# Reordering the opening of a fused spectral-block backward kernel: tables first, half a modulation block first, row scaling on ScalarE, one bias row early

## Chip, cores and metric

One core of a Trainium2 chip. The metric is the device time of one execution in microseconds (us).

## The reference, cut to what matters

The reference computes a block and the gradients of its nine inputs for one `grad_out`. All is bfloat16, S = 2048 rows, D = 512, F = 1792.

```python
mod = (silu(c) @ w_mod)              # six rows of 512: sa, ca, ga, sb, cb, gb
h = layernorm(x) * (1 + ca) + sa
x = x + ga * irfft2(rfft2(h) * (w_r + 1j * w_i))       # spectral part
h = layernorm(x) * (1 + cb) + sb
r = relu(h @ w1 + b1); out = x + gb * (r * r @ w2 + b2) # feed-forward part
# returned: out and the vjp of grad_out for x, w_r, w_i, w1, b1, w2, b2, c, w_mod
```

Two things matter. The gradient of the feed-forward part needs `grad_out @ (w2 * gb).T`, which depends on no row of x. It is ready to be computed as soon as the bias row gb (number 5 of the six) is known. And the spectral part is a chain of stages, each a set of matmuls against transform tables.

## The kernel before

TensorE runs the 224 matmuls `mm<-gT,w2T` of that product as low-priority filler between the stages of the spectral chain. One in-order queue on SyncE (called SPq in the profile) issues all loads, stores and DMA transposes. The opening, with cuts marked:

```python
    for i in range(4):                                   # x rows and the blocks of w_mod
        nc.sync.dma_start(x_sb[:, 4*i:4*i+4, :], x_view[:, 4*i:4*i+4, :])
        if i == 0: load_wm(0)                            # 1 MB: rows 0 and 1
    load_wm(2)
    gT = []
    for b in range(NB):                                  # 4 blocks, but only 2 buffers
        gT.append(w2gp.tile([P, 4, SB], BF16, name="gT", bufs=2))
        for j in range(TB):
            nc.sync.dma_start(gT[b][:, :, j*P:(j+1)*P], g_view[:, TB*b+j, :], transpose=True)
        # [...] w2T after block 0; after block 1 load_wm(1), the 34 loads of w and their write-backs
    build_ta(tc, K, constp, gen, psM)                    # tables
    # [...] the column of silu(c)
    mod_row(1); mod_row(0)
    for q in range(4):                                   # 16 row tiles
        # [...] row statistics
        for j in range(4):
            if j % 2 == 0: nc.vector.tensor_scalar(x_sb[:, t, :], ...)
            else:          nc.scalar.activation(x_sb[:, t, :], ...)
        # [...] h1 = x_sb * ca; first transform psA; its eviction utcs: 1 of 4 on VectorE
    with Priority(tc, LATE):
        nc.sync.dma_start(n1_dram, x_sb)                 # Xs later takes this memory
    build_cd(tc, K, lfp, gen)                            # tables
    for j in (5, 4, 3, 2): mod_row(j)
    # [...] columns of rows 3, 4, 5, then gb2x = 2 * column of row 5
    build_lf(tc, K, lfp, gen)                            # tables LF, most on VectorE
    nc.sync.dma_start(LF_dram, K["LFall"])               # 1.5 MB
    with Priority(tc, LATE):                             # the filler
        for dc in range(4):
            nc.vector.tensor_scalar(w2T[:, dc, :], w2T[:, dc, :], gb2x[:, dc:dc+1], None, op0=ALU.mult)
        # [...] 4 blocks x 14 x 4 matmuls mm<-gT,w2T
    # [...] spectral chain: psB, psC -> Xs (LG transposes of LF_dram between), psG, psT, psY
    nc.sync.dma_start(w1T, B_w1, transpose=True)
    nc.sync.dma_start(w1, w1_view)
    # [...] load_rows(0): second load of x; row statistics; h2T; the feed-forward part
```

Of the kernel before, what the change touches and what calls it, by code (L numbers as in the profile page):

```python
# [9 lines left out]
AF = mybir.ActivationFunctionType  # L10
# [8 lines left out]
D = 512  # L19
# [139 lines left out]



def build_lf(tc, K, cpool, g):
    nc = tc.nc
    V = nc.vector
    ti = g.tile([P, 3], I32, name="lf_ti")
# [9 lines left out]
        V.tensor_scalar(ph[:, i:i + 1], r4, m, a, op0=ALU.mult, op1=ALU.add)  # L175
    sgn = ph[:, 2:3]

    sm = g.tile([P, 6, 4], I32, name="lf_sm")
    nc.gpsimd.iota(sm[:, 0, :], pattern=[[1, 4]], base=0, channel_multiplier=0)
    nc.gpsimd.iota(sm[:, 1, :], pattern=[[-1, 4]], base=3, channel_multiplier=0)  # L180
    nc.gpsimd.iota(sm[:, 2, :], pattern=[[0, 2], [1, 2]], base=0, channel_multiplier=0)
    nc.gpsimd.iota(sm[:, 3, 0:2], pattern=[[1, 2]], base=0, channel_multiplier=0)
    nc.gpsimd.iota(sm[:, 3, 2:4], pattern=[[-1, 2]], base=1, channel_multiplier=0)
    nc.gpsimd.iota(sm[:, 4, 0:2], pattern=[[1, 2]], base=2, channel_multiplier=0)
    nc.gpsimd.iota(sm[:, 4, 2:4], pattern=[[-1, 2]], base=3, channel_multiplier=0)
    mk = g.tile([P, 6, 4], BF16, name="lf_mk")
    V.tensor_scalar(mk[:, 0:5], sm[:, 0:5], sl, None, op0=ALU.is_equal)
    V.tensor_scalar(mk[:, 1], mk[:, 1], sgn, None, op0=ALU.mult)
# [6 lines left out]
    K["LF"] = [LF[:, 2 * gi:2 * gi + 2] for gi in range(8)]  # L195
    K["LFall"] = LF
    for q in range(4):
        kr = g.tile([P, 2, 2, 2, 64], I16, name="lf_kr", bufs=1)
        nc.gpsimd.iota(kr[:, :, :, 0, :], pattern=[[1, 2], [16, 2], [32, 64]], base=2 * q, channel_multiplier=0)
        nc.gpsimd.iota(kr[:, :, :, 1, :], pattern=[[-1, 2], [-16, 2], [32, 64]], base=32 - 2 * q, channel_multiplier=0)  # L200
        if q == 0:
            nc.gpsimd.iota(kr[:, 0, :, 1, 0:32], pattern=[[16, 2], [64, 32]], base=8, channel_multiplier=0)
            nc.gpsimd.iota(kr[:, 0, :, 1, 32:64], pattern=[[-16, 2], [64, 32]], base=56, channel_multiplier=0)
        v = g.tile([P, 2, 4, P], I16, name="lf_v", bufs=1)
        for i in range(2):
            V.tensor_scalar(v[:, i], kr.rearrange("p a h x u -> p (a h) (x u)"), t, ph[:, i:i + 1], op0=ALU.mult, op1=ALU.add)
        if q == 0:
            V.tensor_scalar(v[:, :, 0, 2:64:4], v[:, :, 0, 2:64:4], 512.0, None, op0=ALU.add)
        V.tensor_single_scalar(v, v, 2047, op=ALU.bitwise_and)
        w = g.tile([P, 2, 4, P], BF16, name="lf_w", bufs=2)  # L210
        nc.scalar.activation(w, v, AF.Sin, scale=TWO_PI / 2048, bias=K["npi"])
        n0 = 2 if q == 0 else 0
        for i in range(2):
            for x in range(2):
                V.tensor_tensor(LF[:, 4 * q + n0:4 * q + 4, i, 64 * x:64 * x + 64].rearrange("p n (a b) -> p n a b", b=4),
                                w[:, i, n0:4, 64 * x:64 * x + 64].rearrange("p n (a b) -> p n a b", b=4),
                                mk[:, x, None, None, :].broadcast_to([P, 4 - n0, 16, 4]), op=ALU.mult)
            for h in range(n0):
                V.tensor_tensor(LF[:, h, i, 0:64].rearrange("p (a b) -> p a b", b=4), w[:, i, h, 0:64].rearrange("p (a b) -> p a b", b=4),
                                mk[:, 2 + h, None, :].broadcast_to([P, 16, 4]), op=ALU.mult)  # L220
                V.tensor_tensor(LF[:, h, i, 64:128].rearrange("p (j a b) -> p j a b", j=2, b=2),
                                w[:, i, h, 64:128].rearrange("p (j a b) -> p j a b", j=2, b=2),
                                mk[:, 4, :].rearrange("p (j b) -> p j b", j=2)[:, :, None, :].broadcast_to([P, 2, 16, 2]), op=ALU.mult)
        nc.scalar.activation(LF[:, 4 * q:4 * q + 4, 2, :], LF[:, 4 * q:4 * q + 4, 0, :], AF.Copy, scale=-1.0)
# [4 lines left out]
def spec_f1_row(tc, K, hrow, t, UT, pool, name):  # L229
# [4 lines left out]
        nc.tensor.matmul(ps[:, 2 * c:2 * c + 2, :], lhsT=hrow[:, (c + 2) * P:(c + 3) * P], rhs=K["TA"][:, 1:3], start=False, stop=True)  # L234
    dst = UT[:, :, :, t, :]
    src = ps.rearrange("p c (a b) -> p c a b", b=8)
    if t % 4 == 0:
        nc.vector.tensor_copy(out=dst, in_=src)
    else:
        nc.scalar.copy(out=dst, in_=src)  # L240


def make_ae(nc, pool):
# [190 lines left out]
def kernel(  # L434
# [34 lines left out]
    ccolf = constp.tile([P, 4], FP32, name="ccolf")  # L469
    b1col = constp.tile([P, NFC], FP32, name="b1col")  # L470
    gsc = constp.tile([P, 6, 4], FP32, name="gsc")
    mcol = constp.tile([P, 3, 4], FP32, name="mcol")
    SB_C, CB1_C, GB_C = range(3)
    modb = constp.tile([P, 5, D], BF16, name="modb")
    GA_B, GB_B, CA1_B, CB1_B, SB_B = range(5)
    K = build_basic(tc, constp)
# [9 lines left out]
    nc.vector.memset(ind, 0.0)  # L486
    nc.vector.memset(ind[:, :, 0:1], 1.0)
    gen = tc.alloc_tile_pool(name="gen", bufs=1, side="right")

    gap = tc.alloc_tile_pool(name="gap", bufs=1)  # L490
    gaT = [gap.tile([P, NFC, SB], BF16, name="gab", bufs=4) for b in range(NB)]
# [17 lines left out]
    def load_wm(i):  # L509
        nc.sync.dma_start(wmt[i], wm_view[:, :, 2 * D * i:2 * D * (i + 1)])  # L510

    for i in range(4):
        nc.sync.dma_start(x_sb[:, 4 * i:4 * i + 4, :], x_view[:, 4 * i:4 * i + 4, :])
        if i == 0:
            load_wm(0)
    load_wm(2)
    w2T = w2gp.tile([P, 4, F], BF16, name="w2T")
    gT = []
    for b in range(NB):
# [3 lines left out]
        if b == 0:  # L523
            nc.sync.dma_start(w2T, B_w2, transpose=True)
        if b == 1:
            load_wm(1)
            for gi in range(8):
                nc.gpsimd.memset(Z[gi][:, :, :, DF:FP], 0.0)
                load_w(gi)
                nc.sync.dma_start(wz_dram[:, gi], Z[gi])  # L530
    psF1 = tc.alloc_tile_pool(name="psF1", bufs=2, space=PSUM)
    psM = tc.alloc_tile_pool(name="psM", bufs=2, space=PSUM)
    UT = utcs.tile([P, 4, 16, NT, 8], BF16, name="utcs")
    build_ta(tc, K, constp, gen, psM)
    pv = psM.tile([P, 32], BF16, name="vrow_ps", bufs=1)
    nc.tensor.transpose(pv, vrow, K["ident"][0:32, 0:32])
    nc.vector.tensor_copy(b1col, pv[:, 8:8 + NFC])
    nc.vector.tensor_copy(ccolf, pv[:, 0:4])
    nc.scalar.activation(sigcol, ccolf, AF.Sigmoid)
    sccol = p0.tile([P, 4], BF16, name="sccol")  # L540
    nc.vector.tensor_tensor(sccol, ccolf, sigcol, op=ALU.mult)
    nc.vector.tensor_copy(scf, sccol)
    scb = p0.tile([P, 4, P], BF16, name="scb")
    nc.vector.tensor_copy(scb, sccol[:, :, None].broadcast_to([P, 4, P]))



    srow = p0.tile([1, D], BF16, name="srow")
# [9 lines left out]
        else:  # L558
            nc.scalar.copy(out=srow, in_=ps[0:1, :])

    mod_row(1)
    mod_row(0)


    for q in range(4):
# [8 lines left out]
        nc.vector.scalar_tensor_tensor(out=nb, in0=mv[:, :, 0], scalar=-1.0, in1=i1, op0=ALU.mult, op1=ALU.mult)  # L574
        for j in range(4):
            t = 4 * q + j
            if j % 2 == 0:
                nc.vector.tensor_scalar(x_sb[:, t, :], x_sb[:, t, :], inv1[:, t:t + 1], nb[:, j:j + 1], op0=ALU.mult, op1=ALU.add)
            else:
                nc.scalar.activation(x_sb[:, t, :], x_sb[:, t, :], AF.Identity, bias=nb[:, j:j + 1], scale=inv1[:, t:t + 1])  # L580
# [5 lines left out]

    with Priority(tc, LATE):
        nc.sync.dma_start(n1_dram, x_sb)
    build_cd(tc, K, lfp, gen)
    for j in (5, 4, 3, 2):  # L590
        mod_row(j)
    pm = constp.tile([1, 2], BF16, name="pm")
    nc.vector.memset(pm[:, 0:1], 1.0)
# [10 lines left out]
        for i in range(4):  # L604
            nc.tensor.matmul(psd[:, fs], lhsT=sacol[:, i, e * (i // 2):e * (i // 2) + 1], rhs=K["Cd"][:, i % 2, fs], start=(i == 0), stop=(i == 3))
    nc.vector.tensor_scalar(dcrow, psd, 128.0, None, op0=ALU.mult)
    psc = psM.tile([P, 3, 4], FP32, name="modc_ps", bufs=1)
    for i, row in enumerate((modb[0:1, SB_B, :], modb[0:1, CB1_B, :], modb[0:1, GB_B, :])):
        for cc in range(4):
            nc.tensor.matmul(psc[:, i, cc:cc + 1], lhsT=row[:, cc * P:(cc + 1) * P], rhs=pm[:, 0:1], start=True, stop=True)  # L610
    nc.vector.tensor_copy(mcol, psc)
    gb2x = constp.tile([P, 4], FP32, name="gb2x")
    nc.vector.tensor_scalar(gb2x, mcol[:, GB_C], 2.0, None, op0=ALU.mult)
    build_lf(tc, K, lfp, gen)
    nc.sync.dma_start(Cd_dram, K["Cd"])
    nc.sync.dma_start(LF_dram, K["LFall"])
    gen.release()
# [617 lines left out]
```

## Time and profile before

| | before |
|---|---|
| median of 3 runs | 475.09 us (475.04 to 477.51) |
| span of the profiled execution | 473.4 us |
| TensorE (PE) busy | 432.9 us, 91% |
| VectorE (DVE), ScalarE (ACT) busy | 331.2 us, 257.0 us |
| first filler matmul, last filler matmul | 42.5 us, 137.0 us |

Busy time plus idle time of TensorE is the span, so 473.4 - 432.9 = 40.5 us of idle TensorE is what an edit of the order can win, apart from busy time at a lower clock. A line of a timeline holds start, duration, engine, line, operation; in brackets the idle time just before and what ended it. The prediction shows the opening. Two views also belong here: the stretch 104.6 to 137 us by busy times (length, then PE, PEld, DVE, ACT, POOL, clock, DMA share, GB/s), and the timeline of the loads there (start, duration, engine, line, operation; in brackets the idle time just before and what ended it).

```profile
104.60:137.00 32.40, 28.46 (x179) 15.50 (x172) 21.46 (x46) 22.36 (x40) 0.00 (x0) 1.00 0.49 141
```

### The profile page before, as it was taken

What the parts mean: (1) busy time and instruction counts of PE and PEld (TensorE: products, weight loads), DVE (VectorE), ACT (ScalarE), POOL (GpSimd) and SP (SyncE); (2) the same over time, 40 slices, a digit from 0 to 9 for tenths busy, and PEclk for the clock granted to TensorE, in tenths of its full rate; (3) what the DMA queues carried; (4) which work ended last, traced back from release to release, by engine and by line L of the source; (5) the groups of instructions that cost most, each with busy time, mean ns of one, the idle gap of its engine ahead of it and who ended that gap; (6) DMA issues with size and microseconds to landing.
All of it is one profiled execution on the core that took longest, in us unless ns stands there. A gap on an engine that the chain in (4) does not pass through costs nothing.

```text
span 473.4 us, 7172 instructions
## 1 busy us (share of the span) xinstructions
PE 432.9 (91%) x2485; PEld 218.3 (46%) x2485; DVE 331.2 (70%) x759; ACT 257.0 (54%) x463; POOL 12.7 (3%) x64
## 2 busy tenths in 40 slices
PE   0758999998899999999999798997999999999997
PEld 0434544664454444443454244443555556555442
DVE  5888946983886457677666864733957676769896
ACT  3356745755777148547653764634554546444641
POOL 4121000000000000000000000000000000000000
PEclk9978999999999999999999999998999999999999
DMA  8975667998039639939973696797688549999994
GB/s 275 244 197 163 183 209 222 273 251 300 24 111 370 197 102 208 323 113 172 250 245 115 136 297 232 236 217 240 168 231 292 152 121 317 206 234 292 246 253 137
DMA packets 149371, 101.23 MB, mean 214 GB/s; under 512 B 99282, under 2 KB 133592, under 8 KB 148696
## 3 DMA queue, kind: packets, MB, share of 16 engines
q1 hardware_dynamic: 149336, 100.78, 79.2%
q8 instruction: 19, 0.31, 0.3%
q14 instruction: 16, 0.13, 0.1%
HBM read 35.44 MB, written 41.73 MB: 163 GB/s over the span
## 4 chain that ended last, share of the span: by engine, by line
PE 65%; DVE 11%; DMA 8%; ACT 6%; SPq 5%; issue 2%; POOL 1%; DVEq 0%; ACTq 0%
PE og L803 13%; PE mm L1065 10%; PE mm L780 10%; PE mm L993 10%; PE mm L629 3%; PE psG L302 3%; PE psC L262 2%; PE psT L333 2%; PE psY L347 2%; SPq L770 2%; PE psB L275 2%; DMA o<-gx_dram 2%; DVE l_st L569 2%; DMA n_dram<-x_sb 1%; DMA x<-in_A_x_dram 1%
## 5 line engine op out<-in xcount | busy, mean ns | idle before, releaser
L629 PE MATMUL mm<-gT,w2T 128*128 128x512 bf16 x224 | 54.7, 379 | 2.8 <-DVE gab L632 2.3
L780 PE MATMUL mm<-h2T,w 128*128 128x512 bf16 x224 | 53.3, 379 | 2.2 <-DMA h2T<-h_dram 1.1
L993 PE MATMUL mm<-gab,h_sb 128*128 128x448 bf16 x256 | 52.8, 360 | 0.0
L803 PE MATMUL og<-w,h 128*128 128x512 bf16 x224 | 52.0, 380 | 0.0
L803 PE MATMUL og<-w1T,gab 128*128 128x512 bf16 x224 | 50.3, 379 | 0.0
L1065 PE MATMUL mm<-g_sb,hn 128*128 128x512 bf16 x224 | 50.2, 380 | 0.0
L781 ACT ACTIVATE r<-mm,b1col 128x512 bf16<-128x512 f32 x56 | 37.6, 684 | 13.4 <-PE mm L780 8.6
L993 PEld LDWEIGHTS <-h_sb 128*128 128x128 bf16 x256 | 25.4, 99 | 22.0 <-issue 1.8
L780 PEld LDWEIGHTS <-w 128*128 128x128 bf16 x224 | 21.1, 97 | 30.7 <-issue 8.5
L803 PEld LDWEIGHTS <-gab 128*128 128x128 bf16 x224 | 21.8, 98 | 25.3 <-DVE gab L787 0.5
L629 PEld LDWEIGHTS <-w2T 128*128 128x128 bf16 x224 | 21.2, 97 | 26.4 <-issue 6.8
L1065 PEld LDWEIGHTS <-hn 128*128 128x128 bf16 x224 | 21.5, 98 | 25.5 <-issue 1.3
L803 PEld LDWEIGHTS <-h 128*128 128x128 bf16 x224 | 21.1, 98 | 25.1 <-issue 2.3
L632 DVE CAST gab<-mm 128x512 bf16<-128x512 f32 x28 | 19.2, 686 | 15.1 <-PE mm L629 14.9
L783 DVE TENSOR_TENSOR h<-r 128x1024 bf16<-128x1024 bf16 x28 | 19.3, 690 | 14.2 <-ACT r L781 14.1
L997 ACT CAST gw<-mm 128x448 bf16<-128x448 f32 x16 | 8.5, 532 | 28.5 <-PE mm L993 28.5
L634 ACT CAST gab<-mm 128x512 bf16<-128x512 f32 x28 | 16.3, 582 | 11.3 <-PE mm L629 11.2
L867 ACT CAST o<-og 128x512 bf16<-128x512 f32 x16 | 9.3, 580 | 22.6 <-PE og L803 22.6
L336 ACT ACTIVATE Tsb<-psT 128x512 bf16<-128x512 f32 x32 | 18.3, 601 | 4.9 <-PE psT L333 2.5
L428 DVE SCALAR_TENSOR_TENSOR gm_junk<-wmc,onef,gmbc 128x512 bf16<-128x512 bf16 x24 | 18.0, 750 | 2.9 <-ACT gmbc L417 2.6
L816 ACT CAST G<-og 128x512 bf16<-128x512 f32 x16 | 9.3, 580 | 19.0 <-PE og L803 19.0
L347 PE MATMUL psY<-Tsb,TAT 128*128 128x256 bf16 x128 | 18.1, 272 | 1.5 <-ACT Tsb L336 1.4
(268 smaller groups left out, 763.6 us busy)
## 6 DMA issues: line engine op xcount, KB each, us to landing
h_dram<-h SPq DMA_DIRECT2D x28, 256.0 KB, 3.9
gh_dram<-gab SPq DMA_DIRECT2D x28, 256.0 KB, 4.1
w<-in_B_w_dram SPq DMA_DIRECT2D x2, 1792.0 KB
wm<-in_w_mod_dram SPq DMA_DIRECT2D x3, 1024.0 KB, 6.8
wmc<-in_w_mod_dram SPq DMA_DIRECT2D x12, 256.0 KB, 4.7
out_dram<-gwm SPq DMA_DIRECT2D x12, 256.0 KB, 3.8
wz_dram<-Z SPq DMA_DIRECT2D x8, 258.0 KB, 2.4
xs_dram<-Xs SPq DMA_DIRECT2D x8, 258.0 KB, 2.9
```

Of the source, the lines that this page charges most:

```text
L336: nc.scalar.activation(Tsb, ps, AF.Copy, scale=EF_S)
L347: nc.tensor.matmul(psY[:, H * s:H * s + H], lhsT=K["TAT"][:, s * e], rhs=Tsb[:, H * e:H * e + H], start=(e == 0), stop=(e == 1))
L428: nc.vector.scalar_tensor_tensor(out=junk, in0=wmc[:, i, :], scalar=K["onef"], in1=gmbc, op0=ALU.mult, op1=ALU.mult, accum_out=self.gsc[:, ...
L629: nc.tensor.matmul(ps, lhsT=w2T[:, dc, fc * P:(fc + 1) * P], rhs=gT[b][:, dc, :], start=(dc == 0), stop=(dc == 3))
L632: nc.vector.tensor_copy(out=gaT[b][:, fc, :], in_=ps)
L634: nc.scalar.copy(out=gaT[b][:, fc, :], in_=ps)
L780: nc.tensor.matmul(ps, lhsT=w1[:, dc, (fc + i) * P:(fc + i + 1) * P], rhs=h2T[b][:, dc, :], start=(dc == 0), stop=(dc == 3))
L781: nc.scalar.activation(r[:, i, :], ps, AF.Relu, bias=b1col[:, fc + i:fc + i + 1])
L783: nc.vector.tensor_tensor(h2, r, r, op=ALU.mult)
L803: nc.tensor.matmul(ps, lhsT=lhs(fc), rhs=rhs[:, fc, :], start=(fc == 0 and init is None), stop=(fc == NFC - 1))
L993: nc.tensor.matmul(ps[:, 0:W4], lhsT=h2_sb[:, t, dc * P:(dc + 1) * P], rhs=ghn[t // 4][:, t % 4, fs], start=(t == 0), stop=(t == NT - 1))
L1065: nc.tensor.matmul(ps, lhsT=hns[fc][:, t, :], rhs=g_sb[:, t, :], start=(t == 0), stop=(t == NT - 1))
```

## The change

The intent is to relieve VectorE in the opening and let the filler start sooner. Four parts: the tables are made first of all; of the first w_mod block only the half with row 1 is loaded at first; three of four row scalings and all psA evictions go to ScalarE; row 5 is computed ahead of the other late rows and turned into `gb2x` at once. With them go two smaller edits: row 0, whose half block now lands late, joins the late rows, and the products of row 1 get a higher priority. The core of the diff:

```diff
-    for i in range(4):
+    nc.sync.dma_start(x_sb[:, 0:4, :], x_view[:, 0:4, :])
+    nc.sync.dma_start(wmt[0][:, :, D:2 * D], wm_view[:, :, D:2 * D])
+    for i in range(1, 4):
         nc.sync.dma_start(x_sb[:, 4 * i:4 * i + 4, :], x_view[:, 4 * i:4 * i + 4, :])
-        if i == 0:
-            load_wm(0)
 [...]
         if b == 1:
+            nc.sync.dma_start(wmt[0][:, :, 0:D], wm_view[:, :, 0:D])
             load_wm(1)
 [...]                                  # build_ta, build_cd, iotas of build_lf: before the loads
-            if j % 2 == 0:
+            if j == 0:
                 nc.vector.tensor_scalar(x_sb[:, t, :], ...)
 [...]
-    if t % 4 == 0:
-        nc.vector.tensor_copy(out=dst, in_=src)
-    else:
-        nc.scalar.copy(out=dst, in_=src)
+    nc.scalar.copy(out=dst, in_=src)
 [...]
-    for j in (5, 4, 3, 2):
+    mod_row(5)
+    psc = psM.tile([P, 4], FP32, name="modc_ps", bufs=1)
+    for cc in range(4):
+        nc.tensor.matmul(psc[:, cc:cc + 1], lhsT=modb[0:1, GB_B, cc * P:(cc + 1) * P], rhs=K["ones_col"][0:1, :], start=True, stop=True)
+    gb2x = constp.tile([P, 4], FP32, name="gb2x")
+    nc.vector.tensor_scalar(gb2x, psc, 2.0, None, op0=ALU.mult)
+    for j in (4, 0, 3, 2):
         mod_row(j)
 [...]
-    gb2x = constp.tile([P, 4], FP32, name="gb2x")
-    nc.vector.tensor_scalar(gb2x, mcol[:, GB_C], 2.0, None, op0=ALU.mult)
```

More of the change, by code (lines that the diff above doesn't have):

```diff
@@ L157, in build_cf, with iotas_lf, build_lf @@
     K["Cf"] = Cf
-def build_lf(tc, K, cpool, g):
+def iotas_lf(tc, g):
+    nc = tc.nc
+    sm = g.tile([P, 6, 4], I32, name="lf_sm")
+    nc.gpsimd.iota(sm[:, 0, :], pattern=[[1, 4]], base=0, channel_multiplier=0)
+    nc.gpsimd.iota(sm[:, 1, :], pattern=[[-1, 4]], base=3, channel_multiplier=0)
+    nc.gpsimd.iota(sm[:, 2, :], pattern=[[0, 2], [1, 2]], base=0, channel_multiplier=0)
+    nc.gpsimd.iota(sm[:, 3, 0:2], pattern=[[1, 2]], base=0, channel_multiplier=0)
+    nc.gpsimd.iota(sm[:, 3, 2:4], pattern=[[-1, 2]], base=1, channel_multiplier=0)
+    nc.gpsimd.iota(sm[:, 4, 0:2], pattern=[[1, 2]], base=2, channel_multiplier=0)
+    nc.gpsimd.iota(sm[:, 4, 2:4], pattern=[[-1, 2]], base=3, channel_multiplier=0)
+    krs = []
+    for q in range(4):
+        kr = g.tile([P, 2, 2, 2, 64], I16, name="lf_kr", bufs=4)
+        nc.gpsimd.iota(kr[:, :, :, 0, :], pattern=[[1, 2], [16, 2], [32, 64]], base=2 * q, channel_multiplier=0)
+        nc.gpsimd.iota(kr[:, :, :, 1, :], pattern=[[-1, 2], [-16, 2], [32, 64]], base=32 - 2 * q, channel_multiplier=0)
+        if q == 0:
+            nc.gpsimd.iota(kr[:, 0, :, 1, 0:32], pattern=[[16, 2], [64, 32]], base=8, channel_multiplier=0)
+            nc.gpsimd.iota(kr[:, 0, :, 1, 32:64], pattern=[[-16, 2], [64, 32]], base=56, channel_multiplier=0)
+        krs.append(kr)
+    return sm, krs
+def build_lf(tc, K, cpool, g, sm, krs):
     nc = tc.nc
@@ L176, in build_lf @@
     sgn = ph[:, 2:3]
-    sm = g.tile([P, 6, 4], I32, name="lf_sm")
-    nc.gpsimd.iota(sm[:, 0, :], pattern=[[1, 4]], base=0, channel_multiplier=0)
-    nc.gpsimd.iota(sm[:, 1, :], pattern=[[-1, 4]], base=3, channel_multiplier=0)
-    nc.gpsimd.iota(sm[:, 2, :], pattern=[[0, 2], [1, 2]], base=0, channel_multiplier=0)
-    nc.gpsimd.iota(sm[:, 3, 0:2], pattern=[[1, 2]], base=0, channel_multiplier=0)
-    nc.gpsimd.iota(sm[:, 3, 2:4], pattern=[[-1, 2]], base=1, channel_multiplier=0)
-    nc.gpsimd.iota(sm[:, 4, 0:2], pattern=[[1, 2]], base=2, channel_multiplier=0)
-    nc.gpsimd.iota(sm[:, 4, 2:4], pattern=[[-1, 2]], base=3, channel_multiplier=0)
     mk = g.tile([P, 6, 4], BF16, name="lf_mk")
@@ L197, in build_lf @@
     for q in range(4):
-        kr = g.tile([P, 2, 2, 2, 64], I16, name="lf_kr", bufs=1)
-        nc.gpsimd.iota(kr[:, :, :, 0, :], pattern=[[1, 2], [16, 2], [32, 64]], base=2 * q, channel_multiplier=0)
-        nc.gpsimd.iota(kr[:, :, :, 1, :], pattern=[[-1, 2], [-16, 2], [32, 64]], base=32 - 2 * q, channel_multiplier=0)
-        if q == 0:
-            nc.gpsimd.iota(kr[:, 0, :, 1, 0:32], pattern=[[16, 2], [64, 32]], base=8, channel_multiplier=0)
-            nc.gpsimd.iota(kr[:, 0, :, 1, 32:64], pattern=[[-16, 2], [64, 32]], base=56, channel_multiplier=0)
+        kr = krs[q]
         v = g.tile([P, 2, 4, P], I16, name="lf_v", bufs=1)
@@ L471 @@
     gsc = constp.tile([P, 6, 4], FP32, name="gsc")
-    mcol = constp.tile([P, 3, 4], FP32, name="mcol")
-    SB_C, CB1_C, GB_C = range(3)
+    mcol = constp.tile([P, 2, 4], FP32, name="mcol")
+    SB_C, CB1_C = range(2)
     modb = constp.tile([P, 5, D], BF16, name="modb")
@@ L488 @@
     gen = tc.alloc_tile_pool(name="gen", bufs=1, side="right")
+    psF1 = tc.alloc_tile_pool(name="psF1", bufs=2, space=PSUM)
+    psM = tc.alloc_tile_pool(name="psM", bufs=2, space=PSUM)
+    build_ta(tc, K, constp, gen, psM)
+    build_cd(tc, K, lfp, gen)
+    lf_io = iotas_lf(tc, gen)
     gap = tc.alloc_tile_pool(name="gap", bufs=1)
@@ L530 @@
                 nc.sync.dma_start(wz_dram[:, gi], Z[gi])
-    psF1 = tc.alloc_tile_pool(name="psF1", bufs=2, space=PSUM)
-    psM = tc.alloc_tile_pool(name="psM", bufs=2, space=PSUM)
     UT = utcs.tile([P, 4, 16, NT, 8], BF16, name="utcs")
-    build_ta(tc, K, constp, gen, psM)
-    pv = psM.tile([P, 32], BF16, name="vrow_ps", bufs=1)
-    nc.tensor.transpose(pv, vrow, K["ident"][0:32, 0:32])
-    nc.vector.tensor_copy(b1col, pv[:, 8:8 + NFC])
-    nc.vector.tensor_copy(ccolf, pv[:, 0:4])
-    nc.scalar.activation(sigcol, ccolf, AF.Sigmoid)
-    sccol = p0.tile([P, 4], BF16, name="sccol")
-    nc.vector.tensor_tensor(sccol, ccolf, sigcol, op=ALU.mult)
-    nc.vector.tensor_copy(scf, sccol)
-    scb = p0.tile([P, 4, P], BF16, name="scb")
-    nc.vector.tensor_copy(scb, sccol[:, :, None].broadcast_to([P, 4, P]))
+    with tc.high_priority():
+        pv = psM.tile([P, 32], BF16, name="vrow_ps", bufs=1)
+        nc.tensor.transpose(pv, vrow, K["ident"][0:32, 0:32])
+        nc.vector.tensor_copy(b1col, pv[:, 8:8 + NFC])
+        nc.vector.tensor_copy(ccolf, pv[:, 0:4])
+        nc.scalar.activation(sigcol, ccolf, AF.Sigmoid)
+        sccol = p0.tile([P, 4], BF16, name="sccol")
+        nc.vector.tensor_tensor(sccol, ccolf, sigcol, op=ALU.mult)
+        nc.vector.tensor_copy(scf, sccol)
+        scb = p0.tile([P, 4, P], BF16, name="scb")
+        nc.vector.tensor_copy(scb, sccol[:, :, None].broadcast_to([P, 4, P]))
     srow = p0.tile([1, D], BF16, name="srow")
@@ L559, in mod_row @@
             nc.scalar.copy(out=srow, in_=ps[0:1, :])
-    mod_row(1)
-    mod_row(0)
+    with tc.high_priority():
+        mod_row(1)
     for q in range(4):
@@ L588 @@
         nc.sync.dma_start(n1_dram, x_sb)
-    build_cd(tc, K, lfp, gen)
-    for j in (5, 4, 3, 2):
+    mod_row(5)
[5 more added lines that the diff above has]
+    for j in (4, 0, 3, 2):
         mod_row(j)
@@ L606 @@
     nc.vector.tensor_scalar(dcrow, psd, 128.0, None, op0=ALU.mult)
-    psc = psM.tile([P, 3, 4], FP32, name="modc_ps", bufs=1)
-    for i, row in enumerate((modb[0:1, SB_B, :], modb[0:1, CB1_B, :], modb[0:1, GB_B, :])):
+    psc = psM.tile([P, 2, 4], FP32, name="modc_ps", bufs=1)
+    for i, row in enumerate((modb[0:1, SB_B, :], modb[0:1, CB1_B, :])):
         for cc in range(4):
@@ L611 @@
     nc.vector.tensor_copy(mcol, psc)
-    gb2x = constp.tile([P, 4], FP32, name="gb2x")
-    nc.vector.tensor_scalar(gb2x, mcol[:, GB_C], 2.0, None, op0=ALU.mult)
-    build_lf(tc, K, lfp, gen)
+    build_lf(tc, K, lfp, gen, *lf_io)
     nc.sync.dma_start(Cd_dram, K["Cd"])
```

## The prediction

> **What bounds the kernel now.** I read the page first: PE is busy 91% of a 473.4 us span, so most of the kernel is bound by TensorE, and an edit of the opening can only gain where TensorE is not yet full. The page's 40 slices put that hole in the first 50 us. So I asked next for the busy times by stretch, with borders set at the events that matter. Columns: stretch, its length, busy us and instructions of PE, PEld, DVE, ACT, POOL, then granted clock, DMA share, GB/s.
>
> ```profile
> PE   0758999998899999999999798997999999999997
> 5.40:43.60 38.20, 23.70 (x120) 12.60 (x120) 31.59 (x105) 19.03 (x30) 8.40 (x25) 0.87 0.89 227
> 43.60:57.50 13.90, 11.54 (x70) 6.58 (x70) 12.75 (x44) 8.97 (x13) 1.30 (x4) 1.00 0.61 163
> 57.50:76.10 18.60, 18.24 (x81) 7.61 (x79) 9.47 (x26) 7.70 (x15) 0.35 (x1) 1.00 0.76 269
> 76.10:95.70 19.60, 18.71 (x126) 12.06 (x127) 18.30 (x36) 14.15 (x26) 0.34 (x8) 1.00 0.91 218
> ```
>
> From 5.4 to 57.5 us VectorE is the full engine: 31.59 + 12.75 = 44.3 of 52.1 us, 85%, in a row of small waits. TensorE has 23.7 of the first 38.2, and part of that at half clock. After 57.5 TensorE is full. What fills it is the product gT x w2T (line 629, 224 matmuls): low-priority work with no hurry, stuffed between the stages of the spectral chain. So earlier filler does not by itself end the kernel earlier; the chain beside it has to move too.
>
> That chain I took from the timeline and the chain of waits.
>
> ```profile
> 41.59 0.16 DVE L613 TENSOR_SCALAR gb2x<-mcol 128x4 f32<-128x4 f32 x1
> 46.87 1.28 DVE L624 TENSOR_SCALAR w2T<-w2T,gb2x 128x1792 bf16<-128x1792 bf16 x2
> 57.90 0.33 SPq L616 DMA_DIRECT2D LF_dram<-LF  x1
> 58.41 0.33 SPq L530 DMA_DIRECT2D wz_dram<-Z  x1
> 63.41 5.64 SPq L522 DMA_TRANSPOSE gT<-in_grad_out_dram  x4
> 69.57 0.35 SPq L588 DMA_DIRECT2D n_dram<-x_sb  x1
> 76.13 1.08 ACT L264 CAST Xs<-psC 128x514 bf16<-128x514 f32 x2 [1.30 <-DMA n_dram<-x_sb]
> ```
>
> Read it backwards. At 76.13 the first spectral block leaves PSUM; it had waited for the write of x_sb to DRAM, since Xs lies in memory that x_sb gave up. That write sits in the one in-order DMA queue behind the third block of gT transposes. Those wait for a gT buffer, that is for the first 56 filler matmuls, which end at about 63.4; the queue itself was free from 58.74 on. And the filler starts late because the scaled w2T is complete only at 48.15, as the bias row of g comes last of the six rows. From 76.13 to 95.7 TensorE (18.71 of 19.60) and VectorE (18.30) are both full.
>
> **What the skill says.** The Trainium skill, "VectorE: DVE Perf Modes", section "The perf-mode tier table": a PSUM operand costs a copy a speed tier. The trace agrees: the same 128x512 elements take 684 ns out of PSUM and 415 ns from SBUF. "TensorE: Matmul & The Clock Gate", section "What's actually happening": TensorE falls to half clock after an idle window and needs about 3.4 us of work to leave it. The trace agrees: after the idle stretch from 26 to 30 us the psA matmuls follow each other at 0.21 us, at 24 us they did so at 0.11. "DMA: Bandwidth & Descriptors", section "Measured": 1 MB takes 6.15 us; here the 1 MB blocks of w_mod took 6.8 us to land in the median, among other traffic.
>
> **The change part by part.** Durations are from the groups of the first 60 us.
>
> ```profile
> L578 DVE TENSOR_SCALAR x_sb<-x_sb,inv,l_nb 128x512 bf16<-128x512 bf16 x8 | 3.1, 415 | 0.0
> L238 DVE CAST utcs<-psA 128x512 bf16<-128x512 f32 x4 | 2.7, 684 | 1.2 <-PE psA L234 1.2
> L580 ACT ACTIVATE x_sb<-x_sb,l_nb,inv 128x512 bf16<-128x512 bf16 x8 | 6.1, 805 | 6.3 <-DVE l_nb L574 6.3
> L240 ACT CAST utcs<-psA 128x512 bf16<-128x512 f32 x12 | 6.8, 590 | 7.4 <-PE psA L234 7.2
> ```
>
> Row scaling and evictions: four of eight scalings and all four evictions leave VectorE, 4 x 0.415 + 4 x 0.684 = 4.4 us. ScalarE gets 4 x 0.805 + 4 x 0.590 = 5.6 us; it had 28.0 of 52.1 us busy, so it goes to 33.6, 64%. VectorE goes from 85% to 77%, and now waits more often on ScalarE for a scaled pair.
>
> Tables first: the same instructions, moved. The tables for Cd (4 x 0.37 + 2 x 0.42 = 2.3 us of VectorE, 1.4 of ScalarE) go ahead of the first row scaling, and all index patterns on GpSimd (some 5 us) ahead of the first 1/sqrt. GpSimd stood idle until 8.27, so that costs at most half a us. It removes the waits of the later patterns (16.0 us on GpSimd, off the path).
>
> First w_mod block alone: half a MB less in front of the x rows. At the 345 GB/s of the stretch from 5 to 10 us that is 1.5 us earlier for x, gT and w2T. The half comes back after the second gT block, so the 34 loads of w (one per 0.62 us of queue time in the trace) start at the same time as before, about 29 us. They and their write-backs then take the queue to 57 to 58.5 us, whatever the engines do. This is the new floor.
>
> Bias row early: its four matmuls come second. A walk along the new order of VectorE with the durations above gives: first product h at 16.0 (before: 16.98), the fourth at 24.0 (before: 23.25, here ScalarE is late), the last at 34.65 (before: 36.6), w2T scaled by 36.4 (before: 48.15). Then row 0, whose half block lands only at about 33, holds VectorE until 38.5. The LF tables start at 39.5 instead of 43.6 and end at 52.3 instead of 57.4: 5 us. The filler stands at 44 matmuls at about 55 and reaches 56 at about 57.5.
>
> The queue and the 56th matmul thus meet at about 58. The third gT block goes out at 58.1 instead of 63.4: 5.3 us. The 5.64 of transposes, the 6.4 of the x_sb write, Xs at 70.8. TensorE has 82 filler matmuls in a row for this stretch, 82 x 0.227 = 18.6 us from about 53, so up to 71.6: hardly a gap. Then the 19.6 us to the next stage as before. 160 of the filler matmuls stand ahead of that stage instead of 150, 10 x 0.227 = 2.3 us less for the stretch from 104.6 to 137. There the chain runs through a load of x, row statistics and normalization, so I count a third of it, 0.7. Nothing behind 137 us is touched. Sum: 5.3 + 0.7 = 6.0, and 475.09 - 6.0 = 469.1.
>
> **The rivals.** First, the queue does not hold: the w loads start 1.5 us earlier because the transposes drain earlier, the filler gets its whole lead. TensorE is then some 9 us ahead at 50 us (36 filler matmuls at 0.227 and 8 psB at 0.11), and the kernel takes about 466. For: VectorE loses 4.4 us and w2T is ready 12 us earlier. Against: the loads go out at an even pace in the trace, with the DMA engines at 0.6, which looks like the queue's own issue time.
>
> Second, ScalarE takes VectorE's place. Three scalings of four and all evictions now stand on one in-order engine, a pair of rows costing 2 x 0.59 + 1.5 x 0.8 = 2.4 us, against 22 us for all eight pairs over a window of 25. My walk shows the fourth product already 0.75 us late. If the last product h comes no earlier than 36.6, LF gains only the order of its own work, some 2 us, and the time is about 473.
>
> Third, the new order of the queue: the fourth gT block now stands ahead of the first LG transpose and needs 112 filler matmuls (about 68.5). If it holds LG or shares the engines with the x_sb write, 1 to 3 us go back: about 471.
>
> **Range and chances.** The middle is 469.1. The second and third rival set the upper end, the first the lower: 465.5 to 472.8. Faster by over 2% needs 465.6, that is nearly the whole of the first rival plus the stretch after 104.6: 0.11. Slower by over 2% has no mechanism: 0.01.
>
> **What would show it.** Right: VectorE 4 to 5 us less busy before 57 us; w2T scaled by 37; LF written to DRAM at about 52, or queued behind the w loads to 57; third gT block at 57 to 60 with the queue busy up to it; Xs at 70 to 72; the same distance from Xs to the next stage, 19 to 20 us; everything behind 140 shifted as a whole. Wrong: a third gT block that leaves at 62 or later (the opening did not speed up), a wait of over 2 us of TensorE ahead of Xs, or a stretch after Xs that takes back what the opening gave.

## More of the kernel before

```profile
98.67 8.82 SPq L680 DMA_TRANSPOSE w1T<-in_B_w_dram  x1
107.59 0.52 SPq L657 DMA_DIRECT2D xs_dram<-Xs  x1
108.16 0.42 SPq L683 DMA_DIRECT2D w<-in_B_w_dram  x1
110.77 0.86 SPq L702 DMA_DIRECT2D x<-in_A_x_dram  x2
110.80 0.60 ACT L336 ACTIVATE Tsb<-psT 128x512 bf16<-128x512 f32 x1 [2.39 <-DMA xs_dram<-Xs]
117.26 0.69 DVE L727 TENSOR_TENSOR x<-yg,x 128x1024 bf16<-128x1024 bf16 x1 [2.04 <-DMA x<-in_A_x_dram]
117.99 1.29 DVE L731 BATCH_NORM_STATS2 l_st<-x 128x6 f32<-128x512 bf16 x2
```

TensorE is idle for 32.40 - 28.46 = 3.9 us in the stretch 104.6 to 137 us. The feed-forward part waits for x to be read a second time: that load leaves at 110.77, behind the w1T transposes and the 1.75 MB of w1, and VectorE waits 2.04 us for it. A second link shows here: the last write of Xs leaves at 107.59, also behind w1T. The view of the queue's waits names this write as what held the x load (2.0 us), and ScalarE's first eviction `Tsb` waits 2.39 us for it; TensorE stands 1.41 us behind that eviction, its longest wait in this stretch.

## The result, and the profile after

The changed kernel took 469.69 us in the median (4 runs, 468.04 to 469.82); the kernel before took 475.96 beside it (4 runs). The ratio is 0.9857, 95% interval 0.9819 to 0.9895: within 2%, inside the range, 0.6 us from the predicted 469.1. A ratio here is the mean time of one kernel's runs over that of the other's of the same rounds, so it is not quite the ratio of the quoted medians. The profiled spans are 473.4 and 467.9. Executions over 1.5% slower than the fastest of the same kernel are left out of the means. All outputs are right.

The busy times by stretch after the change (same stretches and columns as before):

```profile
5.40:43.60 38.20, 25.57 (x139) 13.73 (x140) 32.51 (x119) 26.06 (x42) 6.43 (x20) 0.91 0.89 227
43.60:57.50 13.90, 13.18 (x77) 7.09 (x75) 11.89 (x39) 10.21 (x17) 0.35 (x1) 1.00 0.58 158
57.50:76.10 18.60, 16.40 (x76) 7.12 (x75) 6.34 (x10) 6.36 (x11) 0.42 (x8) 1.00 1.04 294
76.10:95.70 19.60, 19.02 (x131) 12.33 (x129) 19.18 (x38) 13.34 (x25) 0.00 (x0) 1.00 1.01 261
104.60:137.00 32.40, 30.96 (x183) 16.66 (x182) 25.78 (x53) 26.06 (x48) 0.00 (x0) 1.00 0.46 160
```

TensorE is busier in the opening and in the last stretch. From 57.5 to 76.1 it has a hole that was not there. VectorE is no less busy up to 57.5 (32.51 + 11.89 = 44.4, before 44.3): it lost 4.4 us of row work and did, in the same time, 2.1 us more of filler evictions and some 3.8 us of table work for a later stage that had come behind 57.5 before. Over the whole kernel it is 325.6, that is 5.6 us less, and ScalarE 263.5, that is 6.5 us more. The row-scaling group of ScalarE shows it (busy us, mean ns, then idle before):

```profile
L589 ACT ACTIVATE x_sb<-x_sb,l_nb,inv 128x512 bf16<-128x512 bf16 x12 | 9.1, 807 | 0.0
```

The w2T scaling from the tile's view (min/median/max ns, first to last start), and the chain to Xs from the timeline:

```profile
L636 DVE TENSOR_SCALAR w2T<-w2T,gb2x x4: 676/677/678, 29.7 to 35.9; 128x1792 bf16<-128x1792 bf16 x4
```

```profile
58.26 0.33 SPq L628 DMA_DIRECT2D LF_dram<-LF  x1
59.14 8.11 SPq L533 DMA_TRANSPOSE gT<-in_grad_out_dram  x4
67.78 0.35 SPq L597 DMA_DIRECT2D n_dram<-x_sb  x1
70.17 6.39 SPq L533 DMA_TRANSPOSE gT<-in_grad_out_dram  x4
74.87 1.08 ACT L270 CAST Xs<-psC 128x514 bf16<-128x514 f32 x2 [2.30 <-DMA n_dram<-x_sb]
```

The scaled w2T is complete at 36.5 (before 48.15), as predicted. The third gT block leaves at 59.14 (before 63.41), but its transposes hold the queue for 8.11 us instead of 5.64, x_sb is written late, and Xs comes at 74.87 instead of 76.13. So only 1.3 us of the opening reached the next stage: psG starts at 94.4, before at 95.7. Yet the filler ends at 129.2, before at 137.0 (start of its last matmul, here and below). The loads behind the chain show where more came from:

```profile
93.55 7.65 SPq L692 DMA_TRANSPOSE w1T<-in_B_w_dram  x1
101.86 0.43 SPq L695 DMA_DIRECT2D w<-in_B_w_dram  x1
105.41 0.81 SPq L714 DMA_DIRECT2D x<-in_A_x_dram  x2
112.70 1.29 DVE L743 BATCH_NORM_STATS2 l_st<-x 128x6 f32<-128x512 bf16 x2
```

The second load of x leaves 5.4 us earlier and its row statistics start 5.3 us earlier. One cause lies in the fence above: the fourth gT block (70.17) now goes out while the queue would wait for the x_sb write anyway. Before, it needed filler matmul 112, which came too late for that, and it stood at 77.56 for 5.1 us between the first LG transpose and the rest. The w1T transposes now leave 5.1 us earlier, and behind them the last write of Xs (101.30 instead of 107.59), for which ScalarE's `Tsb` now no longer waits.

The ledger of idle TensorE, from the busy times (length minus busy; both traces hold the same 2485 matmuls):

| stretch, us | before | after | difference |
|---|---|---|---|
| 0 to 5.4 | 5.4 | 5.4 | 0 |
| 5.4 to 57.5 | 16.9 | 13.4 | -3.5 |
| 57.5 to 76.1 | 0.4 | 2.2 | +1.8 |
| 76.1 to 104.6 | 0.9 | 0.6 | -0.3 |
| 104.6 to 137 | 3.9 | 1.4 | -2.5 |
| 137 to the end | 13.0 | 12.7 | -0.3 |
| all | 40.5 | 35.7 | -4.8 |

Busy time fell by 0.75 (432.93 to 432.18). Together this is the 5.5 us between the spans. A ledger says where time went; it does not say why. That is for the experiments.

### The profile page after: what moved, and what is told of

Same layout as the page of the kernel before. It is cut to its first block, busy times and chain, and to the rows that moved or that the text cites. A ratio compares the mean times of both kernels' runs of the same rounds, so it can differ in the third digit from the quotient of the medians.

```text
span 467.9 us, 7171 instructions
## 1 busy us (share of the span) xinstructions
PE 432.2 (92%) x2485; PEld 218.3 (47%) x2485; DVE 325.6 (70%) x747; ACT 263.5 (56%) x475; POOL 12.2 (3%) x64
## 4 chain that ended last, share of the span: by engine, by line
PE 72%; ACT 7%; DMA 7%; DVE 6%; SPq 6%; issue 2%; POOL 0%; ACTq 0%; DVEq 0%
PE og L815 14%; PE mm L1077 10%; PE mm L792 10%; PE mm L1005 10%; PE mm L641 7%; PE psY L353 3%; PE psG L308 3%; PE psT L339 3%; SPq L782 2%; DMA LG<-LF_dram 2%; DMA o<-gx_dram 2%; PE psC L268 2%; PE psB L281 2%; DMA x_sb<-in_A_x_dram 1%; PE mod_ps L562 1%
## 5 line engine op out<-in xcount | busy, mean ns | idle before, releaser
L795 DVE TENSOR_TENSOR h<-r 128x1024 bf16<-128x1024 bf16 x28 | 19.3, 690 | 12.8 <-ACT r L793 12.7
L799 DVE TENSOR_TENSOR gab<-r,gab 128x1024 bf16<-128x1024 bf16 x28 | 19.2, 685 | 0.0
L1151 ACT CAST gh<-psY 128x512 bf16<-128x512 f32 x16 | 8.6, 593 | 18.4 <-PE psY L353 18.4
```

The lines of the kernel that those rows point to most:

```text
L795: nc.vector.tensor_tensor(h2, r, r, op=ALU.mult)
L799: nc.vector.tensor_tensor(gh, r, gh, op=ALU.mult)
```

## The experiments

All comparisons with the kernel before are on the same chip, five rounds each. They were three calls of four runs, each call on a different chip. There the kernel before took 479.08, 477.62 and 478.82 us in the median, with a spread of 5 to 7 us, so ratios carry an interval of about half a per cent to either side. In the traces of runs 1 to 8, 35 of the 2485 matmul records are missing; I use start times and waits from them, and idle times only to a few tenths. In the edits, ORDER_ONLY stands for a scheduling dependence without a semaphore.

The prediction's own route is the earlier Xs, carried through the chain. After the comparison of the traces two theories stand beside it. In the expectations, A is the filler's head start on TensorE, carried to the end of the filler; the order of the queue is then worth at most 1 us. B is the better place of the fourth gT block in the queue, which the head start makes possible and which brings the loads of w1T and x forward. A rival to all is that VectorE's relief of 4.4 us does it.

### 1. The fourth gT block put back behind the first LG transpose

An order edge in the changed kernel, TensorE's order untouched.

```diff
+        if q == 0:     # gT[3]: its four transposes are to stand behind the first LG transpose
+            [tc.add_manual_dep(g.ins, lg_ins.ins.name, ORDER_ONLY, reason="order") for g in gt_ins[12:16]]
```

> The changed kernel, with the fourth gT block held behind the first LG transpose in the DMA queue, the place it has in the kernel before. TensorE's order is the same instruction for instruction. Theory A (the gain is the filler's head start on TensorE, carried to the end of the filler): at most 1 us lost, about 470. Theory B (the gain is 5.1 us of gT transposes moved out of the queue's busy stretch between the spectral blocks and the second load of x, so that this load comes 5.4 us earlier): the load goes back to about 110 us and 3 to 5 us are lost, about 474.

Measured: 473.77 us (471.16 to 475.09), ratio 0.9882 (0.9828 to 0.9936), span 472.5.

```profile
75.41 5.13 SPq L534 DMA_TRANSPOSE gT<-in_grad_out_dram  x4
96.80 8.90 SPq L695 DMA_TRANSPOSE w1T<-in_B_w_dram  x1
108.74 0.91 SPq L717 DMA_DIRECT2D x<-in_A_x_dram  x2
108.85 0.60 ACT L342 ACTIVATE Tsb<-psT 128x512 bf16<-128x512 f32 x1 [3.17 <-DMA xs_dram<-Xs]
115.71 0.69 DVE L742 TENSOR_TENSOR x<-yg,x 128x1024 bf16<-128x1024 bf16 x1 [0.94 <-DMA x<-in_A_x_dram]
```

Xs and psG came even a little earlier than in the changed kernel (psG 93.5), yet the x load leaves 3.3 us later, VectorE waits for it again, and the filler ends at 132.5 instead of 129.2. TensorE's longest wait is back too: 2.19 us behind `Tsb`, which waits for the last write of Xs (105.80 here, 101.30 in the changed kernel). The granted clock in 104.6 to 137 us is 0.95, in the changed kernel 1.00; by an estimate from these two and the 32.4 us of the stretch, up to 1.6 us of the loss are at the lower clock. So the end doesn't follow Xs, and the place of this block does count: 3 to 4 us in the traces. The timed ratios are less sure: they differ by 0.0025 from the first timing of the changed kernel, inside the interval. This run speaks for B in its mechanism and leaves the size at 1 to 4 us.

### 2. The changed kernel without the early bias row

```diff
-    mod_row(5)
-    [column of row 5 and gb2x here]
-    for j in (4, 0, 3, 2):
+    for j in (5, 4, 0, 3, 2):
         mod_row(j)
+    [column of row 5 and gb2x with the other columns, as in the kernel before]
```

> The changed kernel without the early bias row: the six rows in the order 1, 5, 4, 0, 3, 2 and the scale of w2T taken from the late column product, as before. Theory A: the filler starts at 42 to 44 us as before the change, nearly all of the gain is gone, 474 to 476. Rival (the gain is VectorE's 4.4 us less work in the opening): 471 to 472, since that work is still saved.

Measured: 479.65 us (478.25 to 480.92), ratio 1.002 (0.9973 to 1.0067). The first filler matmul is at 43.5, the third gT block at 63.8, the fourth at 82.3. The other three parts are all there, and nothing is gained: VectorE's relief by itself is refuted as the cause.

### 3. The kernel before with the early bias row alone

```diff
-    for j in (5, 4, 3, 2):
+    mod_row(5)
+    [column of row 5 and gb2x here]
+    for j in (4, 3, 2):
         mod_row(j)
```

> The kernel before with the early bias row alone. Theory A: the filler starts at 36 to 38 us and most of the gain is there, about 471. Rival (VectorE's load in the opening): no gain beyond 1 us, 474 to 475.

Measured: 470.03 us in the median of five executions (467.42 to 471.01; a sixth, 474.77 at a granted clock of 0.977, is left out), ratio 0.9809 (0.9757 to 0.986), span 467.0. My expectation of the filler's start was wrong: VectorE scales w2T only at 39.4 to 43.8, and the first filler matmul is at 42.0. Still, that is over 4 us ahead of the 48.15 of before.

```profile
73.85 5.14 SPq L522 DMA_TRANSPOSE gT<-in_grad_out_dram  x4
95.13 7.87 SPq L684 DMA_TRANSPOSE w1T<-in_B_w_dram  x1
```

The fourth gT block goes ahead of the first LG transpose (79.1), w1T and x come 3.5 and 3.7 us earlier than before, and the filler ends at 130.8. psG, however, starts at 96.0, 0.3 us later than before. The whole gain is there with Xs only 0.6 us earlier and psG no earlier: the prediction's route falls. Most of the gain with the bias row alone is what A expected, though the filler started later than it said.

### 4. The x_sb write at natural priority

```diff
-    with Priority(tc, LATE):
-        nc.sync.dma_start(n1_dram, x_sb)
+    nc.sync.dma_start(n1_dram, x_sb)
```

> The changed kernel with the write of x_sb to DRAM at its natural priority: in the queue it now stands ahead of the third gT block and of the Cd and LF writes. The step of my prediction that Xs waits for this write and that what follows shifts with it: Xs at about 64 instead of 74.9 us and the next stage some 10 us earlier, 461 to 464. Theory A (TensorE is full and the filler only swaps places with the spectral stage): Xs earlier, but the end of the filler at 129 moves by no more than TensorE's remaining idle time before it, 2 to 3 us: 467 to 470.

Measured: 475.55 us (474.75 to 476.73), ratio 0.9938 (0.9893 to 0.9983). Xs is at 65.75 and psG at 85.4, some 9 us earlier than in the changed kernel, and the kernel is slower than the changed one. Both expectations (461 to 464, 467 to 470) missed. The scheduler put only 120 filler matmuls ahead of psG instead of 160. The rest pile up behind: the filler ends at 136.1, and TensorE waits for its evictions (us in total, times, longest):

```profile
PE mm L640 <- DVE gab L643: 4.1, 3, 2.4
```

```profile
111.71 0.69 DVE L738 TENSOR_TENSOR x<-yg,x 128x1024 bf16<-128x1024 bf16 x1 [5.85 <-DMA x<-in_A_x_dram]
```

The second view shows what held VectorE: it stands 5.85 us at the sum that needs x, and the eviction for which TensorE waits 2.4 us comes behind that sum. Xs is 9 us earlier, but x is used at 111.71, in the changed kernel at 111.98: its load stands behind w1T (94.03) and w1 as before. The granted clock in 104.6 to 137 us falls to 0.89. So the earlier gate ran into the load of x. How much of the loss is due to the filler left over, this run can't say.

### 5 to 8. What the other parts are worth, on one chip

The changed kernel again, as control:

> The changed kernel unaltered, as the control for the other three runs on this chip. Both theories: ratio to the kernel before 0.982 to 0.99 as in its first timing (0.9857), the second load of x about 5 us earlier than before and the filler product over about 8 us earlier.

The early bias row alone, again:

> The kernel before with the early bias row alone, repeated beside the changed kernel on one chip. Theory 'the bias row is the whole gain': ratio to before within 0.004 of the control's, either side of it. Rival 'the other three parts (tables first, half block, row scaling on ScalarE) add to it': this kernel is 1 to 3 us slower than the control, ratio 0.988 to 0.992.

The changed kernel with row scaling and evictions divided as before:

```diff
-            if j == 0:
+            if j % 2 == 0:
 [and the eviction branch `t % 4 == 0` on VectorE restored]
```

> The changed kernel with row scaling and evictions back on VectorE. Theory 'the relief of VectorE is off the path once the bias row is early': within 1.5 us of the control; the first product with the filler at 35 to 38 us and the fourth gT block still ahead of the first LG transpose in the queue, 152 filler matmuls instead of 160 ahead of the backward stage. Rival 'VectorE full in the opening is what the change relieves': 2 to 4 us slower than the control, the third gT block 2 to 4 us later.

The kernel before with only that part changed (the reverse of the edit above):

> The kernel before with only the row scaling and the evictions moved to ScalarE. Theory 'only the bias row gains': 0 to 1.5 us from the kernel before, the first filler product at 41 to 43 us, the fourth gT block behind the first LG transpose as before. Rival 'VectorE's 4.4 us count': 2 to 4 us faster than before, filler from 38 to 40 us, third gT block at 60 to 61 us.

| run | median us | ratio to before (95%) | x load | last filler | span |
|---|---|---|---|---|---|
| control | 469.23 | 0.9836 (0.979 to 0.9883) | 105.3 | 128.7 | 468.7 |
| bias row alone | 472.49 | 0.9893 (0.9841 to 0.9945) | 108.5 | 131.8 | 469.6 |
| without the ScalarE part | 471.68 | 0.9911 (0.9858 to 0.9964) | 105.9 | 131.9 | 468.5 |
| ScalarE part alone | 476.44 | 0.9986 (0.9941 to 1.003) | 110.8 | 137.0 | 475.3 |

The ScalarE part alone gives nothing that can be told from zero. With the bias row early, it may add up to 3.6 us by the timing (0.9911 against 0.9836 of some 478), but the intervals overlap and the two spans, of one execution each, are equal. The bias row alone had 0.9809 and 0.9893, the changed kernel 0.9857 and 0.9836: what the other parts add together is smaller than this spread and stays open. On this chip alone, two of the rivals were met by the medians: the bias row alone is 0.0057 behind the control (0.988 to 0.992 was the rival's, within 0.004 the theory's), and the kernel without the ScalarE part is 2.4 us slower (2 to 4 was the rival's, within 1.5 the theory's). So the bias row alone brought about two thirds of the control's gain here (0.0107 of 0.0164). The ScalarE part alone started its filler at 44.6, against 41 to 43 expected.

### 9. One order edge in the kernel before: w1T behind the second load of x

This tests the last link by itself: does the stretch from 104.6 to 137 us hang on when x comes back? TensorE's instructions are the same in the same order.

```diff
+                if b == 0:     # w1T transposes are to stand behind this load of x
+                    tc.add_manual_dep(w1T_ins.ins, x1_ins.ins.name, ORDER_ONLY, reason="order")
```

> The kernel before with one order edge: the transposes of w1T stand behind the second load of x in the queue; TensorE's order is the same instruction for instruction. Theory 'the stretch from 104.6 to 137 us hangs on when x comes back': x load issued at 96 to 100 us instead of 110.8, TensorE's idle time in that stretch 1.5 to 2.5 us instead of 3.9, time 1.5 to 3 us below the kernel before (ratio 0.993 to 0.997). Rival 'the stretch hangs on how much filler is left, x is not waited for': x load as early, idle time and time unchanged within 1 us.

Measured: 473.91 us (472.96 to 475.26), ratio 0.9915 (0.9877 to 0.9953), span 471.2.

```profile
99.65 0.42 SPq L683 DMA_DIRECT2D w<-in_B_w_dram  x1
110.64 0.33 SPq L702 DMA_DIRECT2D x<-in_A_x_dram  x1
111.02 8.49 SPq L680 DMA_TRANSPOSE w1T<-in_B_w_dram  x1
115.84 1.29 DVE L733 BATCH_NORM_STATS2 l_st<-x 128x6 f32<-128x512 bf16 x2
```

```profile
104.60:137.00 32.40, 30.69 (x196) 16.94 (x194) 23.34 (x49) 24.91 (x45) 0.00 (x0) 1.00 0.55 147
```

I had the detail wrong: x left no earlier (110.64). It waited 9.5 us for the last write of Xs, which had left at 100.17 behind w1 and took 10.3 us to land. But the 1.75 MB of w1 had left 8.5 us earlier and were no longer right ahead of it, so x was first used 4.5 us after its issue (115.11) instead of 6.5. The Trainium skill, "DMA: Bandwidth & Descriptors", section "Two DMAs through the same engine are not ordered", says that descriptors of one queue of one DMA engine start in order; the two figures agree with that. Row statistics start 2.15 us earlier, TensorE's idle time in the stretch falls from 3.9 to 1.7, the filler ends 2.0 earlier. The rival of that run, that x is not waited for, is refuted. But x is not the whole of the 2.2 us: 1.2 of them are the wait behind `Tsb` (1.41 before, 0.17 here), which shrank because TensorE came 1.1 us later (psG at 96.8) while `Tsb` started as before (110.66). Over the whole execution TensorE is idle for 40.5 us, as before; the shorter span of this profile is busy time (430.6 instead of 432.9), at a granted clock of 0.989 instead of 0.985. By the timed ratios, one edge in the queue brings about half of what the whole change brings; the profile doesn't show where.

### 10. The same edge in the changed kernel

> The same edge in the changed kernel, TensorE's order again the same. Here the stretch has only 1.4 us of idle TensorE left, so both theories give little: theory 'x' 0 to 1.5 us faster than the changed kernel (ratio to before 0.980 to 0.986), rival 0. If x is the limit of what follows, the h2T matmuls start 1 to 3 us earlier than the 133.1 of the changed kernel.

Measured: 470.56 us (469.17 to 471.78), ratio 0.9841 (0.9803 to 0.9879), span 467.4. The x load leaves at 102.58, row statistics and the h2T matmuls come 0.8 earlier (first one at 125.7, changed kernel 126.5), not the 1 to 3 that I had set for x as the limit. The changed kernel has only 1.4 us of idle TensorE left in that stretch, and the edge can't win it twice. No gain can be told from the control's.

### 11 and 12. The LF write held behind the x_sb write

The prediction's step to Xs failed at the third gT block. This tests why.

```diff
-    nc.sync.dma_start(LF_dram, K["LFall"])
+    lf_ins = nc.sync.dma_start(LF_dram, K["LFall"])
+    tc.add_manual_dep(lf_ins.ins, n1_ins.ins.name, ORDER_ONLY, reason="order")
```

> The changed kernel with the 1.5 MB write of LF held behind the write of x_sb in the queue. The third gT block then has no large write ahead of it. Theory 'the third block took 8.1 us instead of 5.6 because the LF write was still draining': its transposes take 5.6 to 6.4 us, x_sb is written at 65 to 66.5, Xs leaves PSUM at 70.5 to 73 instead of 74.9. Rival 'gT transposes issued behind the w loads are slow as such': 7.5 us or more, Xs at 74 or later. For the time: the scheduler puts 142 instead of 160 filler matmuls ahead of the backward stage here, so, as in the run with the early x_sb write, an earlier Xs should not pay: 468 to 473, ratio 0.985 to 0.995; if the Xs gate were what the end hangs on, 465 to 467.

Measured: 480.15 us in the median of five executions (476.69 to 482.55), ratio 1.004 (0.9991 to 1.0089). A sixth, 484.18 at a granted clock of 0.965, is left out. The profiled one is the fastest.

```profile
58.56 5.64 SPq L533 DMA_TRANSPOSE gT<-in_grad_out_dram  x4
64.33 0.50 SPq L597 DMA_DIRECT2D n_dram<-x_sb  x1
71.11 1.08 ACT L270 CAST Xs<-psC 128x514 bf16<-128x514 f32 x2 [4.10 <-DMA n_dram<-x_sb]
116.10 0.69 DVE L739 TENSOR_TENSOR x<-yg,x 128x1024 bf16<-128x1024 bf16 x1 [6.51 <-DMA x<-in_A_x_dram]
```

```profile
PE mm L641 <- DVE gab L644: 5.9, 2, 5.8
PE psC L268 <- ACT Xs L270: 3.3, 1, 3.3
```

Without the 1.5 MB of LF just ahead, the same four transposes take 5.64 us again, and Xs comes at 71.11: the very step that I had predicted (70.8). The other traces agree: 7.2 to 8.1 us where the block leaves within 0.9 us of the LF write, 6.9 at 1.7 us, 5.5 to 6.1 at 4.3 us or more; in run 4, 1.8 us behind the 2 MB of x_sb, 8.45. And the kernel is as slow as before. The scheduler kept only 142 filler matmuls ahead of psG, TensorE waits 3.3 us at Xs and 5.9 us for a filler eviction, and the fourth gT block is at 76.60. The 5.9 is the load of x again: it leaves at 108.15, VectorE stands 6.51 us for it, and the eviction comes behind. The granted clock is 0.91 in 57.5 to 76.1 us and 0.89 in 104.6 to 137. So the predicted step can be had, and by itself it is worth nothing here; how much of the loss is due to the other order on TensorE, this run can't say.

Both edges together:

> Both edges in the changed kernel: LF write behind the x_sb write, w1T behind the second load of x. If the 1.8 us TensorE loses at Xs and the last idle time before 137 us can both be had, 1 to 3 us faster than the changed kernel (ratio to before 0.978 to 0.984), the fastest of all. If the filler count decides (142 ahead of the backward stage), no faster than the changed kernel: 0.985 to 0.995.

Measured: 474.87 us (471.38 to 475.89), ratio 0.9919 (0.9874 to 0.9965), in the range of the second expectation. That the filler count decided is not shown. What is shown, on one chip: beside run 11 only the w1T edge is new, and it brings 5.3 us (480.15 to 474.87, intervals apart); x leaves at 102.59, VectorE waits 0.35 us for it instead of 6.51, and TensorE's 5.8 us wait is gone. Beside run 10 only the LF edge is new, and it costs 4.3 us by the medians (intervals just overlap), with TensorE now waiting 3.8 us at Xs. No version is clear of the changed kernel's 0.9836 to 0.9857: the lowest ratios are 0.9809 (the bias row alone, 0.9893 when repeated) and 0.9841 (run 10).

## Why the prediction was right or wrong

**The opening was right.** The walk along VectorE's order held to half a us: fourth product h at 23.9 (24.0 predicted), last at 34.24 (34.65), w2T at 36.5 (36.4), filler matmul 56 at 57.5 (57.5). LF ended at about 50.8 (52.3). The first rival fell: the w loads began 1.4 us earlier, but one of them waited, and the last write-back left at 58.77 (before 58.41). The second fell too, as the last product h came as early as my walk had it; its "22 us for all eight pairs" doesn't follow from its own 2.4 us a pair, which give 19. One sign of being right failed: VectorE was to be 4 to 5 us less busy before 57 us and was as busy as before (44.4), because other work moved into the room.

**The step to Xs failed.** I wrote "The third gT block goes out at 58.1 instead of 63.4: 5.3 us. The 5.64 of transposes, the 6.4 of the x_sb write, Xs at 70.8." (The addends as printed give 70.1; the 70.8 also holds half a us of issue gap, and 6.56 us from the write to Xs.) It came at 74.87, 4.1 later. The parts: the block left 1.0 later (59.14), its transposes took 2.5 longer (8.11), and the x_sb write took 0.5 longer from issue to Xs (7.1 against 6.6). The middle one is the LF write: before, it had 5.5 us to drain ahead of the transposes; after, only 0.9. Run 11 shows it. I had carried a duration from a place with an idle queue to one behind 1.5 MB. My own sign for a wrong prediction, over 2 us of TensorE waiting ahead of Xs, came true: 2.2 us. Of the step's 5.3 us only 1.3 stood.

**The third rival had the wrong sign.** I thought the fourth gT block ahead of the first LG transpose would cost 1 to 3 us. Run 1 takes it back behind, and the traces lose 3 to 4 us at the end of the filler. It cost a little of the x_sb write, which run 1 shows as well (psG 1.0 earlier than in the changed kernel, 0.5 earlier than in its control), but it filled a wait of the queue.

**The last term was mis-sized.** For 104.6 to 137 I counted 0.7 us, a third of ten matmuls. The idle time alone fell by 2.5, as the last write of Xs left 6.3 us and x 5.4 us earlier: the wait behind `Tsb` (1.41) is gone, and most of those behind x. Runs 9, 11 and 12 show that this stretch hangs on the place of w1T, the last write of Xs and x in the queue. The end of the filler moved by 7.8: 1.3 from psG, 10 x 0.227 = 2.3 from the ten matmuls done ahead, 2.5 of idle time, and about 0.9 because 8 transform matmuls (0.11 each) now come behind it. These add to 7.0; 0.8 is not placed by them. Counted from the traces up to the last filler matmul, TensorE has 4.9 us less idle time and 2.9 less busy time. 0.9 of the latter are the 8 matmuls; for most of the rest the higher clock of the opening is a candidate (0.93 instead of 0.90 over 5.4 to 57.5 us, by an estimate from these figures 1.6 us).

**So the total was right by two errors that cancel.** 5.3 + 0.7 was predicted. In the ledger's terms the opening gave 3.5, the new wait at Xs took 1.8, the stretch with x gave 2.5, the rest 0.6, and 0.75 came off busy time. "Everything behind 140 shifted as a whole" is only nearly so: about 8.0 ahead at 137 became 5.8 at the end. 0.9 of it are the 8 matmuls just named; eight psC at about 320 us ran slower (1.9 us for what took 1.3); the granted clock in 310 to 335 us is 0.86, before 0.93. The rest is open.

**Which part did it.** The early bias row: without it the gain is gone (run 2), and alone it brings two thirds of the gain or more (runs 6 and 3). The working of the prediction spent most of its steps on the other three. By the ratios, what they add to it lies between nothing and a third of the gain and is not told apart from zero; of them only the ScalarE part was run by itself.

**What the citations in the prediction bear.** The pair 684 and 415 ns differs in type too (float32 in PSUM, bfloat16 in SBUF), so it doesn't test the PSUM operand alone. After the idle stretch up to 29.5 us the half clock lasted to about 39 us in the trace, so the 3.4 us of work are not what this place shows. The 6.15 us for 1 MB are given for DMAs issued from GpSimd and count the DMA engines' busy time; the 6.8 us here are from issue on SyncE to landing. No step of the sum rests on these three.

## What to carry to other kernels

Make what filler work waits for as early as you can: it is worth what it lets the bounding engine do in its holes, and it frees buffers, which moves DMAs to other places in the queue. Follow each of those in the in-order queue to the load that a later stage waits for, and ask of a duration that you carry to a new place what will stand in front of it there. An earlier gate was worth nothing here where the next load did not come earlier with it (runs 4 and 11), so keep a ledger of the bounding engine's idle time by stretch, with what ended each wait, rather than adding up the shifts of a chain.

## What the Trainium skill lacked or had wrong

- "DMA: Bandwidth & Descriptors": no section tells what DMA transposes take right behind a large write. The four transposes of a 512 KB block held the queue for 5.1 to 5.6 us in the kernel before, 5.64 in run 11 with no large write just ahead, and for 8.11 us right behind a 1.5 MB write.
- "DMA: Bandwidth & Descriptors", section "Latency and other measured facts", gives 261 GB/s for transposes with a non-contiguous middle dimension and some 350 to 400 for contiguous ones, with no size. Here 512 KB in 5.64 us of queue time are 93 GB/s, and the 1.75 MB of w1T in 8.49 us some 216 GB/s. These are issue times on the queue, not the engines' busy time, so they don't refute the figure; it doesn't tell what a block costs the queue.
- "Perfetto Trace Analysis", section "Optimization Strategy", advises finding the gaps of the engine to be optimized and making what blocks them start sooner. It lacks the other half: what the engine meets next. In runs 4 and 11 the gate Xs came 9 and 3.8 us sooner than in the changed kernel, and both kernels were slower: VectorE then stood 5.85 and 6.51 us for x, whose load had not come sooner, and only 120 and 142 instead of 160 filler matmuls stood ahead of the next stage.
